# Two one-element loads on ScalarE's queue: issued behind the load of x instead of ahead of it

## The chip, the cores and the metric

The kernel runs on one core of one Trainium2 chip. The metric is the device time of one execution in microseconds (us); lower is better. The time before is the median of three executions, 663.55 us (663.48 to 664.41).

## What is computed

One decode step with one token for each of four sequences (D = 640). The token is normalised once, and two branches use it: attention over a cache of 4,096 keys and values for 32 heads of 128, and a gated MLP (gMLP). The output is their sum with x.

```python
xn  = layernorm(x)                                  # x: 4 x 1 x 640
q   = xn @ wq                                       # 640 x 4096 -> 32 heads of 128
p   = softmax(q . k_cache / sqrt(128))              # k_cache, v_cache: 4 x 32 x 4096 x 128, bf16
a   = (p . v_cache) @ wo                            # 4096 x 640
z   = gelu(xn @ w_in);  z1, z2 = halves of z        # 640 x 1728
g   = w_sp * layernorm(z2) + b_sp                   # w_sp is 1 x 1, b_sp has 1 element
out = x + a + (z1 * g) @ w_out                      # 864 x 640
```

The caches are 134 MB each, and every byte of them is read once: 268 of the 282 MB that the kernel reads.

## The kernel before, in words

**Memory.** One large SBUF tile, `kv`, is cut into five slots of 4 MB (32 KB on each of the 128 partitions). A unit of the key or the value cache is 8 MB (8 heads of one sequence) and takes two slots; there are 16 key units and 16 value units. At the start the slots hold other things: slot 0 holds `wq` and the work space of the first layernorm (x included), slot 2 holds `w_in`, a part of `w_out` and the gMLP's work space. The other `w_out` rows go in three pieces (line 133) into `w_words`, which later serves the transposed keys; line 128 clears it first.

**Queues of transfers.** Three engines issue DMAs, each in its own program order. SyncE's (SP's) queue has nearly all of them: `wq` (line 119), `w_in` (122), two parts of `w_out` (126, 127), pieces 0 and 1 of `w_out` (133), then the key and value units (181) in the order k0, k1, k2, k3, v0, k4, v1, and so on, and `wo` (189). GpSimd issues a small helper load (141) and piece 2. ScalarE issues three loads at the start: x (line 113, 5 KB, to 4 rows), `w_sp` (115) and `b_sp` (116), one element each, and half of the output at the end (618). An instruction that waits holds back all that is behind it on its queue.

**Semaphores of transfers.** The compiler's framework puts the order of each engine together from the dependences, not from the lines alone. It also gives the DMAs of SyncE and ScalarE eight completion semaphores in turn, in one common count. A DMA that takes a semaphore in use waits, on its engine, until the earlier DMA on it has landed. In the compiled program before, the first eight are `w_sp`, `wq`, `b_sp`, x, and then `w_in`, the two parts of `w_out` and piece 0; piece 1 takes the semaphore of `w_sp`, k0 that of `wq`, k1 that of `b_sp`.

**The start.** Line 111 (GpSimd) clears the rows that x is loaded into, so x's DMA waits for it; the two one-element loads wait for nothing, and the framework puts them ahead of x. From x follows the layernorm (lines 205 to 218, VectorE with one step each on GpSimd and ScalarE), its transpose `xnT` (222), q (301, needs `wq` too), its copies and transpose (309, 310) and `qT` (312). After that the gMLP: `xn @ w_in` (338 to 343), gelu (349 to 360), the matmul that spreads the two scalars over the partitions (366), layernorm and gate (371 to 390), and `w_out` (403).

**The main part.** Each key unit is transposed on VectorE (line 425, eight steps of 128 x 2048 words), and multiplied with q on TensorE (436); after four units follows a softmax (443 to 500); each value unit is multiplied on TensorE (509). When the last reader of a slot is done, SyncE's queue issues the next unit into it.

Of the kernel before, what the change touches and what calls it, by code (L numbers as in the profile page):

```python
# [16 lines left out]
def kernel(  # L17
# [19 lines left out]
    nc = tc.nc  # L37
    P = 128
    B, Sq, D = A_x.shape
# [59 lines left out]
    def at_slot(i, n, off=0):  # L99
        return kv[:, i * SL + off:i * SL + off + n]  # L100


    x_flat = A_x.rearrange("b s d -> (b s) d")
# [5 lines left out]
    ln_t = at_slot(0, 8 * D, n_q)  # L109
    XR = 2 * B  # L110
    nc.gpsimd.memset(ln_t[:32, :].bitcast(F32).rearrange("p (a n) -> p a n", a=8)[:, 0::7, :], 0.0)
    x_bf = ln_t[:XR, 0:D]
    nc.scalar.dma_start(out=ln_t[1:XR:2, 0:D], in_=x_flat)
    sb_bf = const.tile([1, 2], BF16)
    nc.scalar.dma_start(out=sb_bf[:, 0:1], in_=B_w_sp)
    nc.scalar.dma_start(out=sb_bf[:, 1:2], in_=B_b_sp[None, :])

    wq = at_slot(0, n_q).rearrange("p (c n) -> p c n", c=DC)
    nc.sync.dma_start(out=wq, in_=A_wq.rearrange("(p c) n -> p c n", c=DC))
# [144 lines left out]
    for q in range(4):  # L264
        nc.gpsimd.tensor_copy(out=SelE[32 * q:32 * q + 32, :, q % 2, :],
                              in_=b8[32 * q:32 * q + 32, 8:8 + HP, None].to_broadcast((32, HP, P // HG)))
# [10 lines left out]
                          in_=ident_f[:].rearrange("p (q x c) -> p q x c", q=2, c=C2))  # L277
# [72 lines left out]
    for q in range(4):  # L350
        rows = slice(32 * q, 32 * q + 32)
        for m, (t, x0, x1, _) in enumerate(z_in[q]):
# [5 lines left out]
            else:  # L358
                for a in range(2):
                    nc.scalar.activation(out=dst[:, a].rearrange("p c (i r) -> p c i r", i=k),  # L360
                                         in_=z[:, a].rearrange("p (r i c) -> p c i r", i=k, c=n), func=ACT.Gelu_apprx_tanh)
# [285 lines left out]
```

## Time and profile before

| | us |
|---|---|
| median of three executions | 663.55 |
| span of the profiled execution, first to last instruction | 661.8 |
| TensorE busy with matmuls | 286.8 |
| VectorE busy | 377.1 |
| ScalarE busy | 74.0 |
| GpSimd busy | 70.1 |
| bytes moved by DMA | 282.60 MB, mean 427 GB/s over the span |
| SyncE's queue of DMAs, share of the 16 DMA engines' time | 98.9% |
| ScalarE's queue of DMAs, the same | 0.0% (28 packets) |

The profile is of one execution. Its own time from outside is not listed apart from its span, so it is taken for one like the three: 663.55 - 661.8 = 1.75 us lie before its first and after its last instruction. The engines' times overlap; none comes near the span. The trace also holds a record of every DMA packet, which says when it began and ended on its DMA engine, its queue and its bytes. The packet clock runs 10.1 us ahead of the span's: the last completion packet of `wq` ends at 27.72 there, and its landing stands at 17.53 in the span; x gives 20.75 and 10.67. All packet times below are already set back by 10.1.

### The profile page before, as it was taken

The numbers are of one execution on the slowest core, as the hardware profiler recorded it, in microseconds if no ns is written. First come the engines' busy times: TensorE is split into PE (matmuls) and PEld (weight loads), VectorE is DVE, ScalarE is ACT, GpSimd is POOL, SyncE is SP. The second block draws the span as 40 slices with busy tenths as digits, with TensorE's granted clock in tenths as the row PEclk, the third lists the DMA queues.
The fourth block names the chain that finished last, engine by engine and source line by source line (L and its number), as shares of the span: only waits on it lengthen the run. The fifth ranks groups of instructions, "written<-read, shape, count | busy, mean of one in ns | idle before, by whom it ended". The sixth has DMA issues, their size and how long they took to land.

```text
span 661.8 us, 5507 instructions
## 1 busy us (share of the span) xinstructions
PE 286.8 (43%) x2291; PEld 107.4 (16%) x2291; DVE 377.1 (57%) x307; ACT 74.0 (11%) x143; POOL 70.1 (11%) x138
## 2 busy tenths in 40 slices
PE   0336555446052456234426065642607245541236
PEld 0221111112011122111102022210202112120113
DVE  5329989766191759718346196764619175971112
ACT  0300000340100000330200000070100000042200
POOL 4620000030200000130300000030110000002300
PEclk9868788669578596676858587665857768766678
DMA  9999999999999999999999999999999999999997
GB/s 370 457 429 428 427 442 437 440 421 428 421 440 433 440 415 446 425 437 436 437 432 432 429 418 437 446 433 440 425 420 436 437 436 417 456 420 437 419 420 289
DMA packets 7132, 282.60 MB, mean 427 GB/s; under 512 B 913, under 2 KB 1308, under 8 KB 1692
## 3 DMA queue, kind: packets, MB, share of 16 engines
q1 hardware_dynamic: 6968, 282.07, 98.9%
q8 instruction: 18, 0.29, 0.2%
q0 software_dynamic: 112, 0.18, 0.1%
q14 instruction: 6, 0.05, 0.0%
q10 hardware_dynamic: 28, 0.01, 0.0%
HBM read 282.25 MB, written 0.01 MB: 426 GB/s over the span
## 4 chain that ended last, share of the span: by engine, by line
DMA 75%; DVE 11%; issue 11%; PE 2%; DVEq 0%; SPq 0%
DMA kv<-in_A_k_cache_dram 59%; DVE w_words L425 11%; DMA kv<-in_A_v_cache_dram 10%; DMA kv<-in_A_wo_dram 4%; DMA kv<-in_A_wq_dram 3%; PE O L509 2%; PE S L436 0%; PE proj L552 0%; DVE o_q L604 0%; DVE o L600 0%; DVEq L425 0%; SPq L189 0%; DVE o_bf L615 0%; SPq L181 0%; PE last L552 0%
## 5 line engine op out<-in xcount | busy, mean ns | idle before, releaser
L425 DVE STREAM_TRANSPOSE w_words<-kv 128x2048 f32<-128x2048 f32 x128 | 282.8, 2275 | 124.8 <-DMA kv<-in_A_k_cache_dram 124.8
L436 PE MATMUL S<-w_words,QZ 128*32 128x512 bf16 x1024 | 186.1, 496 | 258.3 <-DVE w_words L425 258.3
L436 PEld LDWEIGHTS <-QZ 128*32 128x32 bf16 x1024 | 59.7, 110 | 382.9 <-issue 319.5
L509 PE MATMUL O<-kv,Zb 128*32 128x512 bf16 x1024 | 75.0, 458 | 57.4 <-DMA kv<-in_A_v_cache_dram 50.8
L473 ACT ACTIVATE Zb<-w_words,MkE 32x128 bf16<-32x128 bf16 x120 | 61.0, 508 | 117.9 <-PE O L509 104.2
L518 DVE TENSOR_TENSOR om<-O,Mk 128x512 f32<-128x512 f32 x15 | 10.4, 692 | 94.6 <-PE O L509 94.6
L471 POOL TENSOR_SCALAR Zb<-w_words,MkE 32x128 bf16<-32x128 bf16 x60 | 43.1, 718 | 139.3 <-PE O L509 126.9
L509 PEld LDWEIGHTS <-Zb 128*32 128x32 bf16 x1024 | 34.0, 113 | 98.4 <-issue 70.3
L485 ACT ACTIVATE p_bf<-S,negmax 128x1024 bf16<-128x1024 f32 x4 | 4.5, 1114 | 401.8 <-DVE negmax L453 401.8
L469 DVE TENSOR_SCALAR Zb<-w_words,MkE 32x128 bf16<-32x128 bf16 x76 | 24.7, 325 | 2.3
L411 POOL COPY QZ<-qT 32x32 bf16<-32x32 bf16 x16 | 5.0, 315 | 186.4 <-PE S L436 185.9
L519 DVE TENSOR_REDUCE R<-om 128x128 f32<-128x512 f32 x15 | 15.3, 1020 | 0.5
L496 POOL TENSOR_SCALAR rs<-MkB,rowsum 128x4 f32<-128x4 f32 x4 | 1.2, 296 | 112.4 <-ACT p_bf L485 112.4
L491 DVE STREAM_TRANSPOSE w_words<-p_bf 128x1024 bf16<-128x1024 bf16 (+1 forms) x8 | 9.6, 1241 | 5.9 <-ACT p_bf L485 4.1
L542 POOL MEMSET oT<- 128x66 bf16 x4 | 0.5, 146 | 96.5 <-PE proj L552 96.5
L443 DVE TENSOR_REDUCE m<-S 128x1 f32<-128x1024 f32 x4 | 4.9, 1224 | 6.1 <-PE S L436 6.1
L521 DVE TENSOR_SCALAR R<-O,Mk 128x128 f32<-128x128 f32 x1 | 0.4, 351 | 14.0 <-PE O L509 14.0
L531 PE MATMUL misc<-R,SelX 128*128 128x512 f32 x8 | 4.5, 644 | 7.2 <-DVE R L519 5.5
L301 PE MATMUL q<-kv,xnT 128*32 128x512 bf16 x40 | 4.3, 617 | 6.4 <-DVE xnT L222 6.4
L498 PE MATMUL misc<-rs,SelE 128*128 128x4 f32 x8 | 2.4, 365 | 10.4 <-POOL rs L496 10.4
L128 DVE MEMSET w_words<- 128x5440 f32 x1 | 4.6, 4592 | 1.9 <-issue 1.9
L534 DVE TENSOR_TENSOR om<-misc,h 128x512 f32<-128x512 f32 x4 | 2.8, 692 | 4.9 <-PE misc L531 4.9
(107 smaller groups left out, 88.2 us busy)
## 6 DMA issues: line engine op xcount, KB each, us to landing
kv<-in_A_k_cache_dram SPq DMA_DIRECT2D x8, 4096.0 KB, 30.2
kv<-in_A_v_cache_dram SPq DMA_DIRECT2D x1, 6144.0 KB
kv<-in_A_wq_dram SPq DMA_DIRECT2D x1, 5120.0 KB, 16.8
kv<-in_A_wo_dram SPq DMA_DIRECT2D x3, 1280.0 KB
kv<-in_B_w_in_dram SPq DMA_DIRECT2D x1, 2160.0 KB, 22.3
kv<-in_A_v_cache_dram SPq DMA_DIRECT2D x1, 2048.0 KB
kv<-in_A_wo_dram SPq DMA_DIRECT2D x1, 640.0 KB, 23.6
kv<-in_B_w_out_dram SPq DMA_DIRECT2D x1, 320.0 KB
```

Source lines behind the costliest of these rows:

```text
L128: nc.vector.memset(w_words[:, 0:FR * NOUT // 2], 0.0)
L411: nc.gpsimd.tensor_copy(out=QZ[r0:r0 + 32, :, :, :, 8 + 8 * hp], in_=qT[32 * g:32 * g + 32, NE * hp:NE * hp + NE].rearrange("p e a b -> p ...
L425: nc.vector.transpose(kT.rearrange("p (t r) -> p t r", r=32), kw)
L436: nc.tensor.matmul(S_ps[32 * q:32 * q + 32, i], lhsT=QZ[:, b, 2 * kh + w, e, w0:w0 + 32], rhs=kb[:, i, :, e, :, w], start=(b == 0 and k < ...
L443: nc.vector.tensor_reduce(out=m1[:], in_=S_ps[:].rearrange("p i t m -> p (i t m)"), axis=AX.X, op=ALU.max)
L469: nc.vector.tensor_scalar(out=dst, in0=src, scalar1=mk, scalar2=None, op0=ALU.mult)
L471: nc.gpsimd.tensor_scalar(out=dst, in0=src, scalar1=mk, scalar2=None, op0=ALU.mult)
L473: nc.scalar.activation(out=dst, in_=src, func=ACT.Copy, scale=mk)
L491: nc.vector.transpose(pT_t[:, j0:j1, :], blocks)
L509: nc.tensor.matmul(O_ps[32 * q:32 * q + 32, :, :], lhsT=Zb[b % 2][:, w].rearrange("p h c -> p (h c)"), rhs=vv[:, w * 4 * Dh:(w + 1) * 4 * ...
L518: nc.vector.tensor_tensor(out=om4[:], in0=O_ps[:], in1=Mk4[:, :, None].to_broadcast((P, 4, Dh)), op=ALU.mult)
L519: nc.vector.tensor_reduce(out=R, in_=om4[:].rearrange("p c d -> p d c"), axis=AX.X, op=ALU.add)
```

## The change

x's load is given a name, and the two one-element loads get an order edge behind it on ScalarE's queue. Nothing is added or removed.

```diff
-    nc.scalar.dma_start(out=ln_t[1:XR:2, 0:D], in_=x_flat)
+    x_in = nc.scalar.dma_start(out=ln_t[1:XR:2, 0:D], in_=x_flat)
     sb_bf = const.tile([1, 2], BF16)
-    nc.scalar.dma_start(out=sb_bf[:, 0:1], in_=B_w_sp)
-    nc.scalar.dma_start(out=sb_bf[:, 1:2], in_=B_b_sp[None, :])
+    with tc.issue_after(x_in.ins):
+        nc.scalar.dma_start(out=sb_bf[:, 0:1], in_=B_w_sp)
+        nc.scalar.dma_start(out=sb_bf[:, 1:2], in_=B_b_sp[None, :])
```

In the compiled program ScalarE's queue then begins x, `w_sp`, `b_sp`; on every engine the order is otherwise the same. The common count of semaphores turns: the first four are now `wq`, x, `w_sp`, `b_sp`. So piece 1 of `w_out` (SyncE, line 133 before) waits for `wq` to land instead of `w_sp`, k0 waits for x instead of `wq`, k1 for `w_sp` instead of `b_sp`, and k2 for `b_sp` beside its other waits. Lines after the change stand one higher.

## The prediction

> **What bounds the kernel now.** I read the busy time by stretches first, then the chain of waits in order of time, then the timeline of the first 25 us, then the waits of SyncE's queue, and last the trace's packet records.
>
> Busy time by stretches; the last two columns are the DMA engines' busy share and their rate:
>
> ```profile
> core 0: us, PE busy (x) PEld busy (x) DVE busy (x) ACT busy (x) POOL busy (x), PEclk, DMA share, GB/s
> 0.00:30.00 30.00, 6.72 (x103) 3.13 (x103) 13.14 (x17) 6.38 (x12) 16.81 (x57) 0.98 0.97 406
> 30.00:60.00 30.00, 13.50 (x88) 6.04 (x91) 15.81 (x12) 1.78 (x3) 5.10 (x4) 0.67 1.03 444
> 110.00:600.00 490.00, 214.37 (x1678) 78.77 (x1677) 292.95 (x243) 61.27 (x120) 42.09 (x69) 0.72 1.00 432
> 657.00:662.00 5.00, 1.77 (x26) 1.05 (x25) 1.43 (x4) 0.00 (x0) 0.00 (x0) 0.81 0.08 28
> ```
>
> The DMA share is 0.97 to 1.03 from the first stretch on, and VectorE, the busiest engine, has 293 of 490 us. The packet records say it more sharply. From 3.1 us (all 16 engines started) to 654 us, a look every 0.25 us finds 16 packets open, but for 1.25 us at 138 (14 or 15). The 3,456 packets of 65,536 bytes take 2.418 us at the median, 2.415 to 2.428 from the 5th to the 95th percentile. So the time is: the start of the stream (2.2 us), the packets of each engine one behind another, and the work after the last landing. A change counts only if it moves the stream's start, opens a gap in it, or changes the end.
>
> The chain of waits in order of time (start, us, what) starts so:
>
> ```profile
> 0.72 16.81 DMA kv<-in_A_wq_dram
> 17.53 0.02 issue
> 17.55 27.97 DMA kv<-in_A_k_cache_dram
> ```
>
> k0 is issued when wq has landed, and this is no need of data: k0's slots are empty. It is the shared semaphore. The 27.97 us are mostly k0's time behind other packets in the rings, so a later issue of k0 need not be a later landing. That is the main question here.
>
> The timeline of the start (start, us, engine, line):
>
> ```profile
> 0.72 0.54 ACTq L115 DMA_DIRECT2D sb_bf<-in_B_w_sp_dram  x1
> 0.72 0.62 POOL L111 MEMSET kv<- 32x640 f32 x1 [0.29 <-POOLq L631]
> 1.29 0.23 ACTq L116 DMA_DIRECT2D sb_bf<-in_B_b_sp_dram  x1
> 1.56 0.68 ACTq L113 DMA_DIRECT2D kv<-in_A_x_dram  x1
> 6.55 1.74 SPq L133 DMA_DIRECT2D w_words<-in_B_w_out_dram  x2
> 10.72 0.48 DVE L205 CAST kv<-kv 8x640 f32<-8x640 bf16 x1 [4.20 <-DMA kv<-in_A_x_dram]
> 16.28 1.42 DVE L222 STREAM_TRANSPOSE xnT<-kv 32x160 bf16<-32x160 bf16 x4
> 17.55 0.35 SPq L181 DMA_DIRECT2D kv<-in_A_k_cache_dram  x1
> 17.76 4.31 PE L301 MATMUL q<-kv,xnT 128*32 128x512 bf16 x40 [6.40 <-DVE xnT L222]
> ```
>
> x lands at 10.67, and the layernorm's last step ends at 16.28 + 1.42 = 17.70: 7.03 us. q follows at 17.76, only 0.17 us of that later than wq's landing at 17.53.
>
> **The change, part by part.**
>
> *x's issue.* The memset that x waits for ends at 0.72 + 0.62 = 1.34; ScalarE's queue is busy with the two scalars until 1.52, and x starts at 1.56. With x first I put it at 1.40: 0.16 us sooner. The scalars follow at about 2.1 and 2.7, and ScalarE's table load, at 2.28 before, starts near 2.95. It takes 1.28 us and is first needed at 15.00, after 11.44 us of idleness: nothing.
>
> *x's place in the rings.* x moves as four packets of 1,280 bytes on four engines. On three of them the completions come at 7.7, 9.0 and 9.1 us. The fourth is the engine of the scalars: b_sp's two bytes go at 6.0, its completion at 7.56, x at 9.1, x's completion at 10.65, with one wq packet of 1.514 us between any two. With x in front, that engine gives x's data at 6.0 and the completion at 7.6, and the other three decide: x lands at about 9.1, 1.5 us sooner. Bounds: no gain (each item comes a turn later) and 3.0 (all four like the best). I take 1.5, the three undisturbed engines.
>
> The Trainium skill (DMA: Bandwidth & Descriptors, "Queues, rings and completion order") says that an engine drains a whole packet, typically 9 to 17 descriptors, from one queue before it turns to the next. By that rule the scalars and x would go in one turn and x would land where it lands now, which is the second rival below. The trace speaks against it: one item a turn, as just listed. Either way the sum is the same.
>
> *What the sooner x is worth.* The layernorm would end at 9.1 + 7.03 = 16.2, but q also needs wq, at 17.53. q starts at about 17.58 instead of 17.76: 0.18 us. What follows of that is k1's issue (25.10, released by qT), 0.18 sooner; but k1's packets stand in the rings behind k0's, which lands at 45.5. Worth 0. w_in's matmuls start when w_in lands, at 23.5, and gain nothing.
>
> *The scalars' later landing.* Behind x's two items on that engine, four more turns of 1.5 us: 7.6 + 6.1 = 13.7. The first to need them is the matmul of line 366 at 26.68, released by ScalarE. Margin 13 us. k1 and k2, which wait for these semaphores now, are issued at 25.1 and 54.8. Nothing.
>
> *SyncE's queue.* The new wait is the one real risk. Its waits before (line, for what, total us, times, longest):
>
> ```profile
> SPq L181 <- DMA kv<-in_A_wq_dram: 9.2, 1, 9.2
> SPq L181 <- POOL qT L312: 7.1, 1, 7.1
> SPq L133 <- DVE w_words L128: 3.6, 1, 3.6
> ```
>
> The 9.2 us move from k0 to the second issue of line 133, piece 1. Before, piece 1 went right behind piece 0, at 7.54 (6.55 + 0.94 + 0.05), and took 0.75. Now it starts at 17.55, and k0 behind it at 17.55 + 0.75 + 0.05 = 18.35 (18.54 if piece 1 takes the 0.94 of piece 0): 0.8 to 1.0 us later, ending at 18.70.
>
> Is there still work in the rings? k0's first packet ran at 21.4, directly behind the last of the earlier loads on its engine, and seven more engines turned to k0 within 0.3 us; k0's issue had ended at 17.90, so its way into the rings took at most 3.5. The nearest row for that way with nothing ahead is wq: issue ended at 1.11, first packet at 2.2, 1.1 us. So k0 is there at 18.70 + 1.1 = 19.8, and needed at 21.4. Margin 1.6 us, cost 0. The upper end is 0.8 to 1.0 us, if the way took all of the 3.5. A gain from the later issue is excluded, since nothing runs sooner by it. I take 0, since the engines had no gap and wq's row is the only one without a queue.
>
> The Trainium skill (the same page, "Latency and other measured facts") gives an HBM access latency of 0.2 us on average and 2 us at high load. Taken onto wq's row, an estimate, k0 would come at 21.6, and the sum would be 0.2 us more; no row before shows such an increase.
>
> Piece 1 itself: its 12 packets ran from 23.3 to 25.9, behind those of w_in and piece 0. Issued at 17.55 it is in the rings by 19.4, so in the same place, and its readers (line 403) start at 38.3.
>
> **Sum.** Stream's start 0, gap 0, end 0: span 661.8 as before, and with the 1.75 us around it **663.5 us**, the median of the runs shown.
>
> **The rivals.**
>
> 1. *Slower: k0's issue is on the path after all.* Place: SyncE's queue at 17.5 us. Price: 0.8 to 1.0 us, 664.4 to 664.6. It decides from the point where k0 needs over 2.7 us from the end of its issue to its first packet (21.4 - 18.70). For it: the chain runs through k0's issue, and under load b_sp moved only 4.5 us after its issue. Against it: b_sp waited its turn between queues, while k0 stands in the same ring as the packets ahead of it. Even so it stays within 0.2%; beyond, piece 1's issue would have to take over 2 us, against 0.75 to 0.94 in all its rows. Chance 0.10, of which 0.03 beyond.
> 2. *The change does not do what it says: x lands at 10.6 as before*, since it meets the rings a turn later. 663.5 as well. Chance 0.12.
> 3. *Faster: the start is the bound, and x's 1.5 us come through*: 662.0, or 660.5 with 3.0. Against it: wq's landing stops the gain at 0.18, and k1 has 20 us of packets ahead of it. Chance 0.03.
> 4. *The stream's own start moves.* One engine's first wq packet took 2.99 us where the others took 1.64 to 2.32, and it stays some 0.9 us behind. ScalarE no longer issues beside SyncE at 0.72. That could go either way by up to 0.9: 662.6 to 664.4. Chance 0.10, of which 0.02 beyond 0.2% on each side.
>
> **How the numbers follow.** The forecast itself has 0.65; with rival 2 it is 0.77 at 663.5. The three runs lie from 663.48 to 664.41. The range takes in rival 1's upper end (664.6) and rival 4's lower end (662.6), with 0.2 more on each side for a median of another day: 662.4 to 664.8. The measurement of this kernel can tell about 0.2% (1.3 us) from no change. Faster by more: 0.03 + 0.02 = 0.05. Slower: 0.03 + 0.02 = 0.05. Within: 0.90.
>
> **What would show it.** In the profile after, ScalarE's queue has x first at about 1.4, and the cast of line 206 starts near 9.2. SyncE's waits show about 9.9 us for wq at line 134, and none for wq at line 182; k0 is issued near 18.35. If k0 still lands near 45.5 (45.3 to 45.7), the forecast holds; if it lands at 46.3, rival 1 does. q starts at 17.6, on wq instead of xnT. The forecast is wrong if the packet records have a hole near 21 us, or if the units' issues from k2 (54.76) on are shifted by over 1 us.

## The result, and the profile after

The changed kernel takes 664.51 us at the median of 21 runs (664.33 to 665.19), the kernel before 663.48 in 21 runs beside it (663.33 to 664.79): ratio 1.0015, 95% interval 1.0008 to 1.0021. So it is slower by 1.03 us, under 0.2% but clear of the interval. The profiled execution's span is 662.6 us, 0.8 more than before.

The timeline of the start of the changed kernel (start, us, engine, line; lines stand one higher than before):

```profile
1.37 1.19 ACTq L113 DMA_DIRECT2D kv<-in_A_x_dram  x1
2.60 0.28 ACTq L116 DMA_DIRECT2D sb_bf<-in_B_w_sp_dram  x1
2.91 0.26 ACTq L117 DMA_DIRECT2D sb_bf<-in_B_b_sp_dram  x1
9.28 0.48 DVE L206 CAST kv<-kv 8x640 f32<-8x640 bf16 x1 [2.76 <-DMA kv<-in_A_x_dram]
14.84 1.42 DVE L223 STREAM_TRANSPOSE xnT<-kv 32x160 bf16<-32x160 bf16 x4
17.75 1.47 PE L302 MATMUL q<-kv,xnT 128*32 128x512 bf16 x12 [7.84 <-DMA kv<-in_A_wq_dram]
18.53 0.41 SPq L182 DMA_DIRECT2D kv<-in_A_k_cache_dram  x1
```

The change does what it says. x goes first and lands 1.45 us sooner (9.22 instead of 10.67), the layernorm ends at 16.26 instead of 17.70, and q now waits for wq instead of xnT. It starts at 17.75, as before. The last line is the price: k0 is issued at 18.53 instead of 17.55.

The waits of SyncE's queue and the chain of waits show why (first the wait; then start, us, what):

```profile
SPq L134 <- DMA kv<-in_A_wq_dram: 10.2, 1, 10.2
```

```profile
0.72 16.99 DMA kv<-in_A_wq_dram
17.71 0.02 issue
17.73 0.76 SPq L134
18.48 0.04 issue
18.53 27.50 DMA kv<-in_A_k_cache_dram
46.03 0.03 issue
```

wq's landing (17.71) now releases piece 1, and k0 is issued behind it. k0 lands at 46.03, 0.51 later than before; the DMA takes 27.50 us instead of 27.97, so the rings made up for half of the delay and not for all of it. k2 is issued at 55.28 instead of 54.76.

Two stretches around k0's first packets, before and then after (busy by engine, granted clock, DMA share, GB/s):

```profile
19.50:21.00 1.50, 1.50 (x20) 0.57 (x16) 0.00 (x0) 0.00 (x0) 1.50 (x7) 1.00 1.03 412
21.00:22.50 1.50, 1.07 (x12) 0.31 (x5) 0.37 (x1) 0.00 (x0) 1.37 (x5) 1.00 1.26 540
```

```profile
19.50:21.00 1.50, 1.50 (x20) 0.65 (x16) 0.00 (x0) 0.00 (x0) 1.38 (x5) 1.00 0.84 335
21.00:22.50 1.50, 0.69 (x12) 0.21 (x5) 0.69 (x1) 0.04 (x1) 1.42 (x4) 1.00 1.66 620
```

The share falls from 1.03 to 0.84 in the first stretch and rises from 1.26 to 1.66 in the second. This view counts the whole time of a packet in the stretch in which the packet starts, which is how a share can be over 1. So these lines say that k0's first packets start later; they can't show whether an engine stands idle. The packet records can. In those of the changed kernel up to 6 of the 16 engines have no packet open between 21.4 and 22.6 us; before, all 16 have one. And what runs there runs longer. The first k0 packet of an engine takes up to 0.96 us over the undisturbed 2.418, a packet of piece 1 up to 0.28 over its 0.573, while before the change no packet between 20 and 28 us is more than 0.03 over.

The packet times of the changed kernel are set back by 10.0 us, by the same matching as before of wq's last completion packet with its landing. That matching takes the landing to come with the packet, which no run shows. The trace gives packets and instructions in one count of time, in which the span begins at 10.56 before and at 10.46 after. If that count is the right one, every packet time in this document and in the prediction is 0.46 us too late, and every time from an issue to a packet 0.46 too long. Comparisons between such times stay as they are.

For the experiments I add both up: the engines' time without a packet, and the time by which packets exceed what the same size takes undisturbed, from 17 to 30 us after the first wq packet, divided by 16 engines. After the change that is (3.0 + 7.8) / 16 = 0.68 us a mean engine, before 0.01.

### The profile page after: what moved, and what is told of

Read it like the earlier page. It is cut to its first block, busy times and chain, and to the rows that moved or that the text cites. A ratio compares the mean times of both kernels' runs of the same rounds, so it can differ in the third digit from the quotient of the medians.

```text
span 662.6 us, 5508 instructions
## 1 busy us (share of the span) xinstructions
PE 290.8 (44%) x2291; PEld 109.4 (17%) x2291; DVE 377.2 (57%) x307; ACT 73.8 (11%) x143; POOL 70.0 (11%) x138
## 4 chain that ended last, share of the span: by engine, by line
DMA 74%; DVE 12%; issue 11%; PE 2%; ACT 0%; SPq 0%; DVEq 0%; ACTq 0%
DMA kv<-in_A_k_cache_dram 63%; DVE w_words L426 11%; DMA kv<-in_A_v_cache_dram 5%; DMA kv<-in_A_wo_dram 4%; DMA kv<-in_A_wq_dram 3%; PE O L510 1%; DVE w_words L492 0%; DVE Zb L470 0%; DVE m L444 0%; ACT p_bf L486 0%; PE S L437 0%; SPq L134 0%; PE proj L553 0%; DVE o_q L605 0%; PE misc L448 0%
## 5 line engine op out<-in xcount | busy, mean ns | idle before, releaser
L437 PE MATMUL S<-w_words,QZ 128*32 128x512 bf16 x1024 | 188.3, 501 | 254.7 <-DVE w_words L426 254.7
L522 DVE TENSOR_SCALAR R<-O,Mk 128x128 f32<-128x128 f32 x1 | 0.4, 351 | 12.9 <-PE O L510 12.9
L553 PE MATMUL proj<-kv,oT 128*8 128x320 bf16 x54 | 5.2, 332 | 1.6 <-DMA kv<-in_A_wo_dram 1.6
## 6 DMA issues: line engine op xcount, KB each, us to landing
kv<-in_B_w_in_dram SPq DMA_DIRECT2D x1, 2160.0 KB, 22.6
```

The source lines that it names most:

```text
L437: nc.tensor.matmul(S_ps[32 * q:32 * q + 32, i], lhsT=QZ[:, b, 2 * kh + w, e, w0:w0 + 32], rhs=kb[:, i, :, e, :, w], start=(b == 0 and k < ...
L553: nc.tensor.matmul(dst[0:nb, 0:n1 - n0], lhsT=state[("oT", g)][:, c0:c0 + nb], rhs=wo_t[g][:, c, n0:n1], start=start, stop=stop)
```

## The experiments

Theory A: the loss is k0's later issue, which comes from the turn of the semaphores. Theory B: it is the order on ScalarE's queue itself. Theory C: it is piece 1's own late issue. "Before" is measured beside each group of runs; a table of all follows.

**e1: the order of the change without the new wait.**

```diff
-    with tc.issue_after(x_in.ins):
-        nc.scalar.dma_start(out=sb_bf[:, 0:1], in_=B_w_sp)
+    nc.gpsimd.dma_start(out=sb_bf[:, 0:1], in_=B_w_sp)
+    with tc.issue_after(x_in.ins):
         nc.scalar.dma_start(out=sb_bf[:, 1:2], in_=B_b_sp[None, :])
```

> x still goes first on ScalarE's queue, with b_sp behind it; w_sp is issued by GpSimd, whose DMAs have semaphores of their own. So the common count is wq, x, b_sp, ... and piece 1 waits for nothing, while k0 waits for wq as before the change. Theory A (the loss is k0's later issue behind piece 1's new wait): k0 is issued at about 17.7 instead of 18.53, no idle engine near 21 us, 663.5 us as before the change. Theory B (the loss is the order on ScalarE's queue itself: x in the rings ahead of the scalars, and what it does to wq's packets): 664.5 as after the change.

663.59 against 663.46: ratio 0.9999 (0.9990 to 1.0007). x lands at 9.34, as after the change, and k0 is issued with wq's landing, at 17.82. No engine idles. The loss is gone with x still first: theory B falls.

**e2, e3, e8: the order of before, k0 alone later.** One or two small loads on SyncE's queue take wq's semaphore, so that k0 is issued behind them. Piece 1 keeps its early issue.

```diff
+    pad = const.tile([1, 2], BF16)                # e2: one load; e8: tiles of [16, 2]
+    for i in range(2):
+        nc.sync.dma_start(out=pad[:, i:i + 1], in_=B_w_sp)
     load_unit(seq[0])
```

> The kernel before with one more one-element load on SyncE's queue, between piece 1 and k0. It takes wq's semaphore, so it waits for wq in k0's place, and k0 is issued behind it, about 0.4 us later than before (17.95). Order on ScalarE's queue as before. Theory A: first k0 packet came about 2.5 us after the end of its issue in the changed kernel; by that the margin before was 0.8 us, so 0.4 costs little: 663.5 to 663.8. Theory B: 663.5. Theory C (the loss is piece 1's own late issue): 663.5.

> The same with two one-element loads ahead of k0: k0 about 0.75 us later than before (18.3), nearly as late as in the changed kernel (18.53), with x behind the scalars and piece 1 early as before. Theory A: a part or all of the loss, 664.0 to 664.5, and engines without a packet near 21 us. Theories B and C: 663.5.

> As the run with two one-element loads ahead of k0 in the kernel before, but each load now takes 16 rows, which should take longer to issue: k0 about 0.8 us behind wq's landing, as in the changed kernel, with piece 1 issued early and x behind the scalars. Theory A (k0's issue alone): the whole loss, 664.3 to 664.7, with 5 to 9 engine-us lost between 17 and 25 us. Theory C (piece 1's own late issue has a share): clearly less, 663.9 or below.

e2: 663.43, ratio 1.0000 (0.9991 to 1.0009), no idle engine, but 2.1 engine-us of longer packets, 1.4 of it on two of k0's first packets: the edge. e3: 664.17, ratio 1.0007 (0.9998 to 1.0016). e8: 664.34, ratio 1.0006 (0.9997 to 1.0015), its before at 663.61. The intervals of e3 and e8 reach 1, so neither is clear by itself. Counted run by run it is clearer. Over 664 us lie all 21 runs after the change, 10 of 11 of e8, 7 of 11 of e3, 1 of 11 of e2 and none of the 11 of e1; of the kernel before, 20 of 91 beside all these kernels, and 9 of 21 beside e8. The records are in line, too: the same disturbance comes up with k0's delay alone; e8's engines idle for 3.7 and its packets run 9.4 over, as much as after the change. The timeline of e8 at that point:

```profile
17.90 0.82 SPq L193 DMA_DIRECT2D pad<-in_B_w_out_dram  x2
18.77 0.42 SPq L181 DMA_DIRECT2D kv<-in_A_k_cache_dram  x1
```

Theory C is not needed. A small share of piece 1 is not excluded: e8 is 0.73 over its before, the change 1.03, and the interval of e8's ratio is 1.2 us wide.

**e9: both.** e1's edit and e8's two loads.

> The run with w_sp on GpSimd (x first on ScalarE's queue, piece 1 early), and the same two loads of 16 rows ahead of k0. Theory A: the same as the run before it in this call, 664.3 to 664.7: the order on ScalarE's queue makes no difference on either side. Theory B: differs from it by more than 0.5.

664.56, ratio 1.0011 (1.0002 to 1.0019), 0.22 from e8; all 11 runs lie over 664. With k0 late, the order on ScalarE's queue makes no difference that shows, just as without.

**e4: k0 early.** Both scalars on GpSimd, so that no DMA of SyncE's queue up to k0 waits for a semaphore.

```diff
-    with tc.issue_after(x_in.ins):
-        nc.scalar.dma_start(out=sb_bf[:, 0:1], in_=B_w_sp)
-        nc.scalar.dma_start(out=sb_bf[:, 1:2], in_=B_b_sp[None, :])
+    nc.gpsimd.dma_start(out=sb_bf[:, 0:1], in_=B_w_sp)
+    nc.gpsimd.dma_start(out=sb_bf[:, 1:2], in_=B_b_sp[None, :])
```

> x alone on ScalarE's queue, both scalars issued by GpSimd. Then neither piece 1 nor k0 waits for a semaphore, and k0 is issued at about 8.3 us. Theory A: no hole, and nothing more to gain, since the engines had none before either: 663.5. Theory B: 664.5, x being first as after the change.

663.64, ratio 0.9999 (0.9991 to 1.0008), with k0 issued at 8.32. Nothing is to be won past the point where the rings stay full.

**e5: a large dose.** Three small loads; the third moves k0 on to w_in's semaphore.

> The kernel before with three one-element loads on SyncE's queue ahead of k0. The third moves k0 on to the semaphore of w_in, so k0 is issued when w_in lands, near 23.6 us, 6 us later than before. By the 2.5 us from the end of an issue to its first packet, k0's packets start at 26.5: a hole of 5 us on the eleven engines that were ready for it at 21.2 to 21.8, and of 0.8 to 1 us on the three that carry pieces 0 and 1. Theory A1 (the time follows the engines with the most bytes): their 0.8 to 1 us and the refill, 664.5 to 665.5. Theory A2 (the time follows the mean engine): (11 x 5 + 2 x 3 + 3 x 0.9) / 16 = 4 us, 667 to 668.

667.91, ratio 1.0067 (1.0054 to 1.0079): A2, the mean engine, holds, and A1 falls. That the time falls inside the forecast of A2 is in part luck: k0's first packet came at 25.36 instead of 26.5, so the hole is shorter than forecast, and longer packets, which the sum for A2 leaves out, make up for it. The timeline (the small loads, then k0) and two stretches:

```profile
18.79 0.84 SPq L193 DMA_DIRECT2D pad<-in_B_w_sp_dram  x3
23.91 0.36 SPq L181 DMA_DIRECT2D kv<-in_A_k_cache_dram  x1
```

```profile
20.00:25.00 5.00, 4.34 (x85) 2.29 (x79) 1.02 (x2) 0.58 (x1) 4.44 (x19) 1.00 0.77 292
25.00:30.00 5.00, 0.63 (x18) 0.32 (x8) 2.09 (x4) 4.22 (x9) 2.80 (x6) 1.00 0.86 331
```

Shares of 0.77 and 0.86 leave 1.15 + 0.70 = 1.85 us of all 16 engines. That is too little, since packets that start before 30 us and run on count whole in the second stretch, and since a packet that runs longer counts as busy. The packet records give (41.1 + 12.8) / 16 = 3.4 us.

e5 also shows how k0 reaches an engine. When its issue ended at 24.27, 11 engines stood idle, and two more ran dry within 0.9 us. The first k0 packets of these 13 came from 25.36 to 25.67. The other three still carried piece 1. One of them went on to k0 without a gap at 26.07. The other two ended their last piece packets at 25.7 and 25.9, then stood idle, and got k0 only at 26.96 and 27.76: 2.7 and 3.5 us after the end of the same issue.

| kernel | k0's issue behind the first issue that wq releases, us | engines idle, engine-us | packets longer, engine-us | sum / 16 | span of this execution, us | median of all, us | over its before |
|---|---|---|---|---|---|---|---|
| before | 0 | 0.0 | 0.2 | 0.01 | 661.8 | 663.48 | |
| e1 | 0 | 0.0 | 0.2 | 0.01 | 662.0 | 663.59 | 0.13 |
| e4 | k0 at 8.32 | 0.0 | 0.7 | 0.04 | 661.9 | 663.64 | 0.18 |
| e2 | 0.32 | 0.0 | 2.1 | 0.13 | 661.5 | 663.43 | -0.03 |
| e3 | 0.61 | 0.4 | 5.9 | 0.40 | 661.8 | 664.17 | 0.71 |
| after | 0.80 | 3.0 | 7.8 | 0.68 | 662.6 | 664.51 | 1.03 |
| e8 | 0.87 | 3.7 | 9.4 | 0.82 | 662.8 | 664.34 | 0.73 |
| e9 | 0.87 | 3.8 | 6.7 | 0.65 | 662.7 | 664.56 | 0.95 |
| e5 | k0 at 23.91 | 41.1 | 12.8 | 3.37 | 666.1 | 667.91 | 4.45 |

The lost engine time is that of one execution, so it is best set beside the span of that execution. Over the 661.8 of before, the span grows by 0.8 after the change, 1.0 in e8, 0.9 in e9 and 4.3 in e5, 1.2 to 1.4 times the loss; what makes the rest is open. e3 does not fit: its profiled execution, one of its faster ones (663.70 from outside), lost 0.40 and is no longer than before.

**e6, e7, e10: an attempt at a better version, and a miss.** Pieces 0 and 1 lie on few engines; they were given to GpSimd's queue, in the kernel before (e6) and after (e7).

```diff
-    load_piece(nc.sync, 0)
-    load_piece(nc.sync, 1)
...
         load_piece(nc.gpsimd, 2)
+        load_piece(nc.gpsimd, 0)
+        load_piece(nc.gpsimd, 1)
```

> The kernel before with pieces 0 and 1 of w_out issued by GpSimd, behind piece 2, instead of SyncE. SyncE's queue then has eight DMAs of the common count up to k0, so k0 waits for no semaphore and is issued at about 3 us; and the pieces need not share the same three engines. Before, the engines ended between 652.3 and 656.4 us after the first wq packet, so at most 1 us lies between the mean and the last. Theory A1: if the pieces fall on other engines, 662.5 to 663.3. Theory A2: 663.5, since the bytes are the same.

> The changed kernel with the same edit: x ahead of the scalars, pieces 0 and 1 issued by GpSimd, so that nothing on SyncE's queue waits for wq and k0 is issued at about 3 us. Theory A: the loss of the change is gone, the same time as the run with this edit alone (662.5 to 663.5). Theory B (order on ScalarE's queue costs by itself): 1 us above that run.

669.80, ratio 1.0097 (1.0084 to 1.0111), and 669.95, ratio 1.0098 (1.0083 to 1.0114): 6 us slower, and the same for either order on ScalarE's queue, which is once more against theory B. In e6 w_in's packets of 17,280 bytes take 0.914 us on the mean instead of 0.644. Two things differ from before, the pieces' queue and k0's issue at 2.94 us. e10 is e6 with two small loads ahead of k0, which bring k0 back behind wq:

> Pieces 0 and 1 issued by GpSimd as in the run that gave 669.8, but with two one-element loads on SyncE's queue, issued before wq lands, so that k0 falls on wq's semaphore again and is issued near 17.6 instead of 3 us. If the 6.3 us there came from k0's early issue, this gives 663.5 to 664.5. If they came from the pieces going through GpSimd's queue beside w_in's packets, it stays at 668 to 670, with w_in's packets of 17,280 bytes stretched over 0.644 us as there.

669.89, ratio 1.0096 (1.0079 to 1.0113), k0 issued at 18.35, w_in's packets at 0.905: k0's early issue is not the reason, the move of the pieces is. It changes two things that no run separates: the queue, and the time. In e6 the pieces' packets run from 16.4 us on, beside those of w_in; before, they came from 21.4 on, mostly behind them. From 10 to 30 us all packets of e6 together run 4.2 us a mean engine over their undisturbed time; the rest of the 6.3 us, and why the packets are stretched, is open. No version here beats the kernel before.

## Why the prediction was wrong, point by point

**What held.** x's issue was put at 1.40 and came at 1.37; x's landing at 9.1, and came at 9.22. SyncE's wait for wq moved from k0 to piece 1, 10.2 us against about 9.9. q waits for wq, and x's 1.45 us are worth nothing: e1, which has them without the late k0, is within 0.13 of before. The scalars' later landing cost nothing that shows. That the DMA stream sets the time is what all runs show.

**The step that failed** is k0's way into the rings: "So k0 is there at 18.70 + 1.1 = 19.8, and needed at 21.4. Margin 1.6 us, cost 0." The 1.1 us came from wq, which found empty rings. After the change k0's issue ended at 18.94, and on the six engines that stood idle its first packets came from 21.63 to 22.52: 2.7 to 3.6 us. The run that bears on it is e5, with both ways behind one issue: 1.1 to 1.4 us on the 13 engines that stood idle at its end or soon after, 2.7 and 3.5 on two that worked on for 1.4 us or more and still stood idle before k0 came. So wq's row was a true one for another state, an engine without work. What makes the way longer on an engine that has work is open. The nearest row by state was in the prediction too: the bound of 3.5 us from k0 before, with packets running ahead of it. That this bound was met without a gap was read as a margin. e2 shows that there was little: a delay of 0.32 already makes packets longer, and 0.61 opens a gap.

Of the two rules weighed, the latency of the Trainium skill (DMA: Bandwidth & Descriptors, "Latency and other measured facts", 2 us at high load) gave an estimate of 21.6 for k0's first packet; it came at 21.63. The closeness is in part luck, since the issue itself ended 0.24 later than the estimate took it (18.94, not 18.70). No run shows that this latency is the reason. The sum that went with it, 0.2 us, was five times too small.

**The second miss is within the same term.** The cost was counted as the hole alone: a change was to count "only if it moves the stream's start, opens a gap in it, or changes the end". The larger part is what goes with the hole, 7.8 engine-us of longer packets against 3.0 of idle engines; in e6 no engine idles, and longer packets go with 6.3 us. The trace of before had shown that packets can run longer: at the stream's start the first 16 wq packets together run 10.6 us over 16 x 1.514.

**Rival 1** is what happened, in place (SyncE's queue at 17.5 us), in price (664.4 to 664.6 forecast, 664.51 measured), and nearly in its point of decision (2.7 us from the end of the issue to the first packet; 2.7 to 3.6 measured). The price is in part luck. It was the delay of the issue, 0.8 to 1.0 us, come through whole; in fact k0 landed only 0.51 later (46.03, between the 45.5 of the forecast and the 46.3 named for rival 1), k2 was issued 0.52 later, and idle engines and longer packets make the 0.68 of the table. Its chance of 0.10 was too low: against it stood the row of the wrong state, and that k0 is in the same ring as the packets ahead of it, which did not bring it sooner. Rival 2 fell, since x did land sooner. Rival 3 fell by e1 and e4. Rival 4 is not seen: wq lands at 17.71 after the change, and at 17.80 in e1, which loses nothing; and the first 16 wq packets run 12.9 us over 16 x 1.514 after the change, as they do in e2, which loses nothing either.

## What to carry to other kernels

Moving one DMA in program order can move every wait that is handed out by count: compare the semaphores of the two compiled programs, and follow the wait that lands on a long transfer to what is queued behind it. Where a stream of transfers bounds a kernel, an issue must stand in the rings well before they run dry; take the time from issue to first packet from a transfer that was issued while the engines still had work, not from the first one of the program. A gap costs more than its length: the packets around it ran longer in every run here that had one.

## What the runs showed of the hardware

- From the end of an issue on SyncE's queue to the first packet on an engine: 1.1 us with empty rings (wq at the start); in e5 1.1 to 1.4 us on the 13 engines that had no work at the end of k0's issue or ran out of it within 0.9 us, but 2.7 and 3.5 us on two that ran out of it after 1.4 and 1.6 us. After the change, 2.7 to 3.6 us on the six engines that ran dry, all of which had worked on for over 2 us. By the trace's own count of time each of these is about 0.46 shorter.
- A restart is dear: 16 first packets run 10.6 us over in sum at the stream's start, and the refill in e5, where 12 of the 16 engines start within 0.25 us, costs 12.8.
- With loads of 12,800 and 15,360 bytes a row on GpSimd's queue, running beside w_in's on SyncE's queue, w_in's packets of 17,280 bytes took 0.914 us on the mean instead of 0.644 (e6; 0.905 in e10).
- Of the runs of the kernel before beside all these kernels, 20 of 91 lie above 664 us, up to 665.1; of e1 and e4 none of 22. Whether before now and then meets the same gap, being near the edge, is open: no such run was profiled.
